# The first block of x loaded with two tokens per partition, and the token order restored by strided copies

## The chip, the cores and the metric

The kernel is one program on one core of a Trainium2 chip. The core has a matrix engine (PE in the profile, with its weight loads shown apart as PEld), a vector engine (DVE), a scalar engine with function tables (ACT), a general engine (POOL) and a sequencer that mostly issues transfers (SP). Sixteen DMA engines move data between the chip's memory (HBM) and the on-chip buffer. The metric is the device time of one execution in microseconds (us).

## The reference

One input x of 2048 tokens by 512 features goes through two branches, and a gate per token mixes them.

```python
x = A_x
g = _sigmoid((x * gate_w).sum(-1, keepdims=True))
a = _A_ref(x, A_wq, A_wk, A_wv, A_wo, A_beta)          # 32 heads of 16, four segments of 512 tokens
b = _B_ref(x, B_w_gate, B_w_up, B_w_down)              # gelu(x @ w_gate) * (x @ w_up) @ w_down, 1792 wide
return g * a + (1 - g) * b
```

Branch A is causal attention inside each segment of 512 tokens, plus a linear memory that each later segment reads from the segments before it. Branch B is a gated feed-forward layer. All inputs are bf16.

## The kernel before, in words

The tokens are worked in four segments (0 to 3) of 512. For a segment the kernel needs x with features on the partitions (the tile `xT`), from which the matrices K, Q, V, the gate product G and the up product U are made; attention is made of score matmuls (`qk`), exponentials on ACT (`exp`, of 128x2048 each), masks on POOL (`msk`) and value matmuls (`pv`); the down products (`D`, `R`) end a segment, and `fin` scales and stores.

Segments 1 to 3 get `xT` by transposing transfers. Segment 0 gets it in another way, because it is the start of the program: two transfers `x0_0` and `x0_1` (line 622) bring 256 tokens each into `xin`, a part of the tile `hT[1]`, with tokens on the partitions. Slot `a` of partition `p` holds token 256u + 128a + p. PE transposes the 128x128 pieces (`x0t0a_u`, `x0t0b_u`, `x0t1_u`, line 648) into PSUM, and three copies for each u (`x0ev0a_u`, `x0ev0b_u`, `x0ev1_u`, lines 653 to 656) put them into `xT[0]`: `x0ev0a_0`, `x0ev0a_1` and `x0ev1_0` run on DVE, the other three on ACT. The weights of K come meanwhile in three pieces: `w_wk0` and `w_wk1` from ACT's queue, `w_wk2` from SP's.

While the first transfers are on their way, PE runs eight matmuls on constants (`warm0` to `warm7`, line 639), seven of 512 columns and one of 256. Then come the transposes and the K matmuls of segment 0, which are cut so that a matmul needs one feature block and one half of the tokens (`K0_t.i`).

`xin` has a second use. `gmul0` (DVE) multiplies it by the gate weights, and `gsum0_0` to `gsum0_3` (lines 813 to 819) sum over the features: slot `a` gives the gate logits of 128 tokens in column `a` of `glog`. `gexs0` (ACT) takes the exponential, `gts0` (DVE) makes the reciprocal that `fin` scales with, `exsT0` (POOL, 16 small copies) puts it where `GdT0` (DVE) needs it, and `norm0_t` (DVE) scales the attention output with that.

The order of the work is written out by hand: the dictionary `ORDER` has one list of task names for each engine and one for SP's transfers, and each engine works through its list strictly. A task is given to ACT or to DVE by the list it stands in. A planner inside the kernel (`Sched`) walks the lists to assign PSUM banks and derives from the tasks' reads and writes which semaphores each instruction waits for. Its table `LANDING` holds the landing times that it assumes for the first transfers.

Of the kernel before, what the change touches and what calls it, by code (L numbers as in the profile page):

```python
# [13 lines left out]
ALU = mybir.AluOpType  # L14
# [80 lines left out]
    ),  # L95
    "act": (
# [370 lines left out]
def _build(es, nc, A_x, A_wq, A_wk, A_wv, A_wo, A_beta, B_w_gate, B_w_up, B_w_down, gate_w, out):  # L467
# [165 lines left out]
    xdma(1, 3, 4)  # L633
    wdma(("wg", 1), SP, wg[:, :, half:DF], wgr[:, :, half:DF], 1100000)

    for i in range(8):
        gw = Grp(banks)
        n = 256 if i == 7 else 512
        task(f"warm{i}", PE, [Instr(lambda e, gw=gw, n=n: e.matmul(  # L639
# [626 lines left out]
```

## Time and profile before

| quantity | value |
|---|---|
| time, median of 3 executions | 261.67 us |
| the three executions | 261.67, 906.1 and 261.62 us |
| span of the profiled execution | 657.2 us (10358 instructions) |
| busy on DVE, ACT, POOL in it | 190.9, 213.9 and 100.9 us |
| bytes moved in it | 18.43 MB in 32780 packets |

The span runs from the first to the last instruction of one execution that the profiler recorded; the page gives no other time for that execution. It is not an execution like the two near 261.6 us. Whatever is read off PE's rows therefore has to be brought to the pace of the median, while transfers and the other engines have their own clocks. In the views that follow, an instruction's row has its start, its duration, its engine, its line, the operation and its operands; `x8` at the end counts merged instructions. In rows of groups, the numbers behind the bar are busy us and the mean ns of one. In rows of stretches (such as 3.00:4.00) the last two numbers are the share of the 16 DMA engines that is busy and the GB/s that they move.

### The profile page before, as it was taken

Reading aid. Unit: us, or ns where it says so; the run is one execution under the profiler, and the core shown is the slowest. Engines: PE = TensorE matmul, PEld = TensorE weight load, DVE = VectorE, ACT = ScalarE, POOL = GpSimd, SP = SyncE. Lnnn points to the kernel's source line nnn. Section 1 sums busy time; section 2 is a strip of 40 time slices with the busy share of each in tenths; the row PEclk is TensorE's granted clock in tenths of the full one; section 3 lists DMA queues with packets and bytes.
Section 4 is the critical chain, followed back from the end, with each engine's and each line's share of the span. In section 5 each row is a group of like instructions: output and inputs, shape, how many; then the busy total and the mean of one; then the engine's idle time right before and its main releaser. Section 6 shows DMA issues by size and latency. Waiting matters only on the chain.

```text
span 657.2 us, 10358 instructions
## 1 busy us (share of the span) xinstructions
PE 654.3 (100%) x4644; PEld 225.9 (34%) x4644; DVE 190.9 (29%) x353; ACT 213.9 (33%) x184; POOL 100.9 (15%) x260
## 2 busy tenths in 40 slices
PE   9999999999999999999999999999999999999998
PEld 5222432323332323432332332334234233242344
DVE  0333344433333003442522003334432100233221
ACT  2434334347204223334224223334421332232210
POOL 4014024030003011213000110120220002203100
DMA  9000401000600300200001201001000000200001
GB/s 267 14 6 20 137 17 49 1 1 1 177 0 17 50 1 9 50 0 1 1 17 33 33 1 36 7 1 41 1 9 17 1 1 0 58 9 1 1 1 33
DMA packets 32780, 18.43 MB, mean 28 GB/s; under 512 B 20576, under 2 KB 32736, under 8 KB 32736
## 3 DMA queue, kind: packets, MB, share of 16 engines
q1 hardware_dynamic: 31904, 16.99, 10.6%
q10 hardware_dynamic: 832, 0.79, 0.4%
q8 instruction: 36, 0.59, 0.4%
q14 instruction: 8, 0.07, 0.0%
HBM read 9.84 MB, written 2.10 MB: 18 GB/s over the span
## 4 chain that ended last, share of the span: by engine, by line
PE 100%; DVE 0%; issue 0%
PE psW L545 39%; PE psW L547 26%; PE psW L1092 15%; PE psXALL L924 7%; PE psW L972 6%; PE psXALL L547 2%; PE psW L980 2%; PE psXALL L545 1%; PE psW L639 1%; PE psXALL L648 0%; PE psW L890 0%; PE psXALL L843 0%; DVE obf L1158 0%
## 5 line engine op out<-in xcount | busy, mean ns | idle before, releaser
L930 ACT ACTIVATE pt<-psXALL 128x2048 bf16<-128x2048 f32 x64 | 120.2, 1878 | 257.7 <-PE psXALL L924 254.0
L933 POOL TENSOR_SCALAR_AFFINE_SELECT pt<-pt 128x256 bf16<-128x256 bf16 x128 | 54.1, 431 | 366.2 <-ACT pt L930 361.7
L1092 PE MATMUL psW<-wd,hT 32*128 32x512 bf16 x576 | 90.3, 827 | 0.0
L545 PE MATMUL psW<-xT,wu 128*128 128x512 bf16 x122 | 76.3, 819 | 0.0
L545 PE MATMUL psW<-xT,wg 128*128 128x512 bf16 x118 | 74.3, 827 | 0.0
L1071 DVE TENSOR_TENSOR hT<-psW,hT 128x512 bf16<-128x512 f32 x56 | 38.2, 690 | 122.6 <-PE psW L545 69.5
L547 PE MATMUL psW<-xT,wg 128*32 128x512 bf16 x424 | 65.8, 822 | 0.0
L547 PE MATMUL psW<-xT,wu 128*32 128x512 bf16 x408 | 64.2, 821 | 0.0
L924 PE MATMUL psXALL<-qT,kpad 32*128 32x320 bf16 (+3 forms) x512 | 46.2, 475 | 0.0
L986 DVE STREAM_TRANSPOSE tb<-psW 128x512 f32<-128x512 f32 x32 | 22.7, 714 | 80.4 <-PE psW L980 80.4
L972 PE MATMUL psW<-pt,vaug 128*17 128x192 bf16 (+3 forms) x512 | 46.0, 526 | 0.0
L1092 PEld LDWEIGHTS psW<-wd,hT 32*128 32x128 bf16 x576 | 27.5, 169 | 53.4 <-issue 52.9
L1121 DVE TENSOR_SCALAR ost<-psW,omgt 128x512 bf16<-128x512 f32 x10 | 7.5, 750 | 116.4 <-PE psW L545 106.4
L933 POOL TENSOR_SCALAR_AFFINE_SELECT ptl<-ptl 128x512 bf16<-128x512 bf16 x32 | 21.6, 676 | 115.6 <-ACT ptl L930 114.0
L972 PEld LDWEIGHTS psW<-pt,vaug 128*17 128x17 bf16 x512 | 25.4, 157 | 31.6 <-issue 26.7
L545 PE MATMUL psW<-wv,xT 128*128 128x512 bf16 x54 | 35.1, 810 | 0.0
L545 PEld LDWEIGHTS psW<-xT,wg 128*128 128x128 bf16 x118 | 18.9, 166 | 45.4 <-issue 41.8
L545 PEld LDWEIGHTS psW<-xT,wu 128*128 128x128 bf16 x122 | 18.8, 161 | 45.2 <-issue 44.1
L1055 ACT ACTIVATE hT<-psW 128x512 bf16<-128x512 f32 x28 | 16.5, 598 | 54.0 <-PE psW L547 40.2
L924 PEld LDWEIGHTS psXALL<-qT,kpad 32*128 32x128 bf16 x512 | 12.0, 111 | 60.5 <-issue 53.3
L547 PEld LDWEIGHTS psW<-xT,wg 128*32 128x32 bf16 x424 | 19.6, 166 | 32.3 <-issue 30.2
L547 PEld LDWEIGHTS psW<-xT,wu 128*32 128x32 bf16 x408 | 18.5, 159 | 32.6 <-issue 30.7
(124 smaller groups left out, 550.5 us busy)
## 6 DMA issues: line engine op xcount, KB each, us to landing
out_dram<-ost SPq DMA_DIRECT2D x15, 128.0 KB, 1.8
wg<-in_B_w_gate_dram SPq DMA_DIRECT2D x2, 896.0 KB, 6.9
wu<-in_B_w_up_dram SPq DMA_DIRECT2D x2, 896.0 KB, 6.0
wd<-in_B_w_down_dram SPq DMA_DIRECT2D x2, 896.0 KB, 7.2
phkt<-in_A_x_dram SPq DMA_DIRECT2D x3, 512.0 KB, 4.0
vlow<-vaug SPq DMA_DIRECT2D x8, 136.0 KB, 2.7
hT<-in_A_x_dram SPq DMA_DIRECT2D x2, 256.0 KB, 3.8
wo<-in_A_wo_dram SPq DMA_DIRECT2D x1, 512.0 KB, 4.0
```

Of the source, the lines that this page charges most:

```text
L545: return e.matmul(view(), lhsT, rhs, start=first, stop=last)
L547: r = e.matmul(view()[c:c + 32, :], lhsT[:, c:c + 32], rhs, start=first, stop=last, tile_position=(0, c))
L924: instrs.append(Instr(lambda e, g=g, lhs=lhs, rhs=rhs, c0=c0, ncol=ncol: e.matmul(X[g][:, c0:c0 + ncol], lhs(32 * g), rhs(32 * g), start=T ...
L930: exp_task(s, f"exp{s}_{t}{name}", [Instr(lambda e: e.activation(dst[:], XALL[:, :].rearrange("p (g c) -> p g c", g=4), ACTF.Exp, scale=AT ...
L933: task(f"msk{s}_{t}{name}", POOL, [Instr(lambda e, view=view, pat=pat, base=base: e.affine_select(out=view, in_=view, compare_op=ALU.is_ge ...
L972: instrs.append(Instr(lambda e, t=t, q=q, kb=kb, slot=slot, c0=c0: e.matmul(gp.f32()[32 * q:32 * q + 17, 128 * kb + 64:512], Vaug[sl][:, k ...
L980: instrs.append(Instr(lambda e, t=t, q=q, kb=kb, c0=c0: e.matmul(gp.f32()[32 * q:32 * q + 17, 128 * kb:128 * kb + 64], Vlow[j][:, kb, 4 * ...
L986: task(f"pvt{s}_{t}_{j}", DVE, [Instr(lambda e: e.transpose(Tb[:, j, :], gp.f32()[:, :]), [gp.key], [("Tb", j)], 0.71)], grp=gp)
L1055: lambda e, g=g, ft=ft, s=s: e.activation(hT[s % 2][:, ft, :], g.f32()[:, :], ACTF.Gelu_apprx_tanh),
L1071: task(f"Um{s}_{ft}", DVE, [Instr(lambda e, g=g, ft=ft: e.tensor_tensor(hT[sl][:, ft, :], g.f32()[:, :], hT[sl][:, ft, :], ALU.mult), [g.k ...
L1092: return Instr(lambda e: e.matmul(gs[tile].f32()[:, :], a[32 * r:32 * r + 32, :], b[32 * r:32 * r + 32, :], start=False, stop=False, tile_ ...
L1121: DVE: [Instr(lambda e: e.tensor_scalar(ost[:], g.f32()[:, :], omgt[:, gt:gt + 1], None, ALU.mult), rd, wr, dve_t(512, ap=True))]}, grp=g))
```

## The change

- `x0_0` and `x0_1` put two consecutive tokens into each partition: slot `a` of partition `p` now holds token 256u + 2p + a. What a partition receives is then one run of 2 KB in HBM, where it was two runs of 1 KB.
- The six copies out of PSUM write with a step of two elements, so that `xT[0]` has its tokens in the old order.
- The gate sums of segment 0 go to spare columns 12 to 15 of `glog`. Four new transfers `gl00`, `gl01`, `gl10` and `gl11` on SP's queue, of 64 partitions by 2 single float32 values, bring them into columns 0 to 3 in the old order; `gexs0` waits for all four.
- The warm-up matmuls are seven of 512 columns; the one of 256 columns is gone.
- All five lists of `ORDER` are new. PE's list has the same tasks without `warm7`; SP's has the four new transfers. ACT's list gets 26 tasks that were on DVE and gives 17 to DVE. `LANDING` stays.

```diff
-            lambda u=u: A_x[0, u * 256:(u + 1) * 256, :].rearrange("(a p) d -> p a d", p=P), [],
+            lambda u=u: A_x[0, u * 256:(u + 1) * 256, :].rearrange("(p a) d -> p a d", p=P), [],
...
-    for i in range(8):
+    for i in range(7):
         gw = Grp(banks)
-        n = 256 if i == 7 else 512
-        task(f"warm{i}", PE, [Instr(lambda e, gw=gw, n=n: e.matmul(
-            gw.f32()[:, 0:n], ones[:, 0:128], ones[:, 0:n], start=True, stop=True),
-            [], [gw.key], mm_t(n))], grp=gw, bias=5000.0 - i)
+        task(f"warm{i}", PE, [Instr(lambda e, gw=gw: e.matmul(
+            gw.f32()[:, :], ones[:, 0:128], ones[:, :], start=True, stop=True),
+            [], [gw.key], mm_t(512))], grp=gw, bias=5000.0 - i)
...
-        dst = xT[0][:, k0:k0 + nk, 256 * u:256 * u + 256]
+        dst = xT[0][:, k0:k0 + nk, 256 * u:256 * u + 256].rearrange("p k (c a) -> p k a c", a=2)
...
-            DVE: [Instr(lambda e, dst=dst, src=src: e.tensor_copy(dst, src), [key], wr, dve_t(256 * nk, 2))]}))
+            DVE: [Instr(lambda e, dst=dst, src=src: e.tensor_copy(dst, src.rearrange("p k (a c) -> p k a c", a=2)), [key], wr, dve_t(256 * nk, 2))]}))
...
+        gl, gk = (glog[:, 12:16], ("glog", 3)) if s == 0 else (glog[:, s4], ("glog", s))
...
+                DVE: [Instr(lambda e, a=a: e.tensor_reduce(gl[:, a:a + 1], xt[:, a, :], AXX, ALU.add),
...
+        if s == 0:
+            for h in range(2):
+                for a in range(2):
+                    dma(f"gl{h}{a}", SP, lambda h=h, a=a: glog[a:P:2, h:4:2],
+                        lambda h=h, a=a: glog[64 * h:64 * h + 64, 12 + a:16:2],
+                        [gk + (c,) for c in (a, 2 + a)], [("glog", 0, h, a), ("glog", 0, 2 + h, a)], 60000, nonc=True)
```

The lists of ACT and SP in the part of segment 0 that has the gate's tasks, before and after:

```diff
 act
-Q0_3ev K0_2ev exp0_0A0 gexp K0_3ev exp0_0B0 Vev0_2 exp0_0L gsum0_1 exp0_0A1 Q1_1ev exp0_0B1 Q1_3ev gexs0
-exp0_1A0 pke0_1 exp0_1B0 Gev1_2 exp0_1A1 pqe1_0 exp0_1B1
+Q0_3ev kl0_11 exp0_0A0 Vev0_3 Vev0_2 exp0_0B0 Vev0_1 exp0_0L gexp gsum0_0 exp0_0A1 Q1_2ev exp0_0B1 pke0_1 exp0_1A0
+Q1_0ev exp0_1B0 gexs0 pqe1_0 exp0_1A1 pqe1_1 exp0_1B1
 sp
-w_wg1 Vlo0_1 Vlo0_0 pkT0_0 pkT0_2 pkT0_1 pkT0_3 w_wu0 w_wu1
+w_wg1 gl11 pkT0_0 Vlo0_1 gl01 gl10 Vlo0_0 gl00 pkT0_1 pkT0_3 pkT0_2 xt1 w_wu0 w_wu1
```

More of the change, by code (lines that the diff above doesn't have):

```diff
@@ L651, in _build @@
             for k in range(nk) for a in range(2)])
-        dst = xT[0][:, k0:k0 + nk, 256 * u:256 * u + 256]
+        dst = xT[0][:, k0:k0 + nk, 256 * u:256 * u + 256].rearrange("p k (c a) -> p k a c", a=2)
         wr = [("xT", 0, k0 + k, u) for k in range(nk)]
         S.add(Task(f"x0ev{nm}_{u}", {
-            ACT: [Instr(lambda e, dst=dst, src=src: e.activation(dst, src, ACTF.Copy), [key], wr, act_t(256 * nk))],
-            DVE: [Instr(lambda e, dst=dst, src=src: e.tensor_copy(dst, src), [key], wr, dve_t(256 * nk, 2))]}))
+            ACT: [Instr(lambda e, dst=dst, src=src: e.activation(dst, src.rearrange("p k (a c) -> p k a c", a=2), ACTF.Copy), [key], wr, act_t(256 * nk))],
+            DVE: [Instr(lambda e, dst=dst, src=src: e.tensor_copy(dst, src.rearrange("p k (a c) -> p k a c", a=2)), [key], wr, dve_t(256 * nk, 2))]}))
     c = [Instr(lambda e: e.memset(maskc[0][:], 0.0), writes=[("c", "mask", 0)], est=0.1)]
@@ L815, in prep @@
                 ACT: [Instr(lambda e, a=a: e.activation(xt[:, a, :], xt[:, a, :], ACTF.Copy,
-                                                        accum_out=glog[:, 4 * s + a:4 * s + a + 1]),
-                            [("gprod", s)] + xkeys, [("glog", s, a), ("gjunk", s, a)], 0.64)],
-                DVE: [Instr(lambda e, a=a: e.tensor_reduce(glog[:, 4 * s + a:4 * s + a + 1], xt[:, a, :],
-                                                           AXX, ALU.add),
-                            [("gprod", s)] + xkeys, [("glog", s, a), ("gjunk", s, a)], dve_t(512))]}))
+                                                        accum_out=gl[:, a:a + 1]),
+                            [("gprod", s)] + xkeys, [gk + (a,), ("gjunk", s, a)], 0.64)],
+                DVE: [Instr(lambda e, a=a: e.tensor_reduce(gl[:, a:a + 1], xt[:, a, :], AXX, ALU.add),
+                            [("gprod", s)] + xkeys, [gk + (a,), ("gjunk", s, a)], dve_t(512))]}))
+        if s == 0:
[4 more added lines that the diff above has]
+                        [gk + (c,) for c in (a, 2 + a)], [("glog", 0, h, a), ("glog", 0, 2 + h, a)], 60000, nonc=True)
         exp_task(ph, f"gexs{s}", [Instr(lambda e: e.activation(exs[:, s4], glog[:, s4], ACTF.Exp),
-                                        [("glog", s, a) for a in range(4)], [("exs", s)], 0.25)])
+                                        [("glog", s, a) + u for a in range(4)
+                                         for u in (((0,), (1,)) if s == 0 else ((),))], [("exs", s)], 0.25)])
         task(f"gts{s}", DVE, [
```

186 rows, old and new, of the table ORDER are left out of this document.

## The prediction

> **What bounds the kernel now.** The page came first, for the span and the engines' shares.
>
> ```profile
> span 657.2 us, 10358 instructions
> ...
> PE 654.3 (100%) x4644; PEld 225.9 (34%) x4644; DVE 190.9 (29%) x353; ACT 213.9 (33%) x184; POOL 100.9 (15%) x260
> ...
> PE 100%; DVE 0%; issue 0%
> ```
>
> The span, 657.2 us, is the only time of its own that the profile gives for this execution; nothing in it shows what lies around. It is 2.5 times the median, 261.67 us, and PE is busy for 654.3 us of it, which no run of 261.67 us can hold. So I take PE's rows at a smaller pace: 261.67 / 654.3 = 0.40 of their duration at most, if PE never rested in the median run. DVE's 190.9 and ACT's 213.9 us do fit into 261.67 (73 and 82%), so their rows and those of the transfers are used as they stand. The sum below is a difference: it is made on the profile's rows, and added to the median.
>
> Next I read the chain of work that ended last, and the timeline of the first microseconds, for what starts the real work.
>
> ```profile
> 0.85 4.58 PE psW L639 x8
> 5.44 1.11 PE psXALL L648 x8
> 6.54 1.48 PE psW L545 x5
> ...
> 28.56 5.94 PE psW L545 x10
> ```
>
> ```profile
> 0.82 0.96 SPq L582 DMA_DIRECT2D hT<-in_A_x_dram  x2
> ...
> 4.27 0.10 PEld L639 LDWEIGHTS psW<-const-bfloat16-1.0 128*128 128x128 bf16 x1 [0.39 <-issue]
> 4.89 1.34 PEld L648 LDWEIGHTS psXALL<-ident,hT 128*128 128x128 bf16 x8 [0.52 <-DMA hT<-in_A_x_dram]
> ```
>
> ```profile
> L582 SPq DMA_DIRECT2D hT<-in_A_x_dram x2: 450/452/454, 0.8 to 1.3; - x2
> ...
> DMA to landing us min/median/max: 3.5/3.8/4.1
> ```
>
> The first block was issued at 0.82 and landed 3.5 us later, at 4.3; the second at about 1.3 + 4.1 = 5.4. The trace puts the weight load at 4.89 down to that transfer, but it comes 0.62 us after the one at 4.27, as each warm-up's load does, and the warm-ups end at 5.43: in the profile PE, not the transfer, set the start. At 0.40 of their duration the warm-ups end by 0.85 + 4.58 x 0.40 = 2.7, and at twice that by 4.5. So in the median run the landing at 4.3, or the warm-ups very near it, starts the transposes. Everything behind them (K, scores, exponentials) follows in PE's order; time won there is won at the end unless a later wait takes it.
>
> **The packets.** The change makes 256 packets of 1 KB into 128 of 2 KB. No row has a 2-KB packet; the nearest are those of `w_g`, of 1.75 KB, alone on the engines at 15 to 17 us.
>
> ```profile
> 2.00:3.00 1.00, 1.00 (x3) 0.26 (x2) 0.00 (x0) 0.30 (x2) 0.85 (x4) 1.00 0.70 152
> 3.00:4.00 1.00, 1.00 (x3) 0.47 (x2) 0.00 (x0) 0.00 (x0) 1.00 (x1) 1.00 1.09 366
> 4.00:5.00 1.00, 1.00 (x3) 0.20 (x2) 0.00 (x0) 0.00 (x0) 1.00 (x2) 1.00 1.08 378
> ...
> 15.00:16.00 1.00, 1.00 (x4) 0.47 (x3) 0.00 (x0) 0.69 (x1) 0.00 (x0) 1.00 0.94 351
> 16.00:17.00 1.00, 1.00 (x3) 0.33 (x2) 0.00 (x0) 0.00 (x0) 0.00 (x0) 1.00 0.94 364
> ```
>
> With 1-KB packets the engines move 366 and 378 GB/s, with 1.75-KB ones 351 and 364: larger packets move no more bytes. The page "DMA: Bandwidth & Descriptors" of the Trainium skill (Specifications) speaks against this edit too: it asks for 512 B or more for line rate, so 1 KB is enough; by it alone the gain is nil, and the trace agrees.
>
> What can change is whose bytes go first. By 4.00 us 152 + 366 = 518 KB had moved, and `x0_0` is 262 of them; the other 256 KB (K's first weights, and part of what is behind) took 256 / 366 = 0.70 us of the engines. If all of it were to go behind `x0_0`, the block would land 0.7 us sooner; if none, no sooner. A loss I exclude, since the bytes and their rate stay. I take 0.2 us, nearer to nil, because the rate is the row that is known and the order among queues is not. The second block gains at least as much, or waits no longer; its landing at 5.4 lies behind the first K matmuls, so it must follow for the gain to hold, and it is in the same form.
>
> **The copies out of PSUM.** Six copies get a step of two elements.
>
> ```profile
> L656 DVE COPY xT<-psXALL 128x256 bf16<-128x256 bf16 x2 | 0.6, 292 | 8.2 <-PE psXALL L648 8.2
> L656 DVE COPY xT<-psXALL 128x512 bf16<-128x512 bf16 x1 | 0.4, 415 | 0.0
> L655 ACT ACTIVATE xT<-psXALL 128x256 bf16<-128x256 bf16 x2 | 0.8, 385 | 6.2 <-PE psXALL L648 6.2
> L568 DVE CAST qT<-psXALL 128x512 bf16<-128x512 f32 x1 | 0.7, 692 | 5.4 <-PE psXALL L545 5.4
> ```
>
> On DVE 256 more elements cost 415 - 292 = 123 ns, about 2 elements a ns, and the constant part is 169 ns. The nearest row that does not run so is the cast of 512, 692 ns: (692 - 169) / 512 = 1.02 ns an element. At that pace 256 elements take 169 + 261 = 430 ns and 512 take 692: 0.14 us more for `x0ev0a_0` and `x0ev0a_1` each, 0.28 for `x0ev1_0`. The least is nil. The page "VectorE: DVE Perf Modes" (What auto-detection actually checks) wants a step of one in every tensor for two elements a cycle, so by it the higher price is the right one. On ACT I book nothing: 385 ns for 256 elements is already slower than one a ns, so that a step has nothing to take away. The first copy is on the path (PE's first K matmul reads it); the later two have K's matmuls of the other half beside them, 1.48 us for five in the profile, still 0.6 us at 0.40. So 0.14 us is booked, with 0 and 0.14 + 0.14 + 0.28 = 0.56 as ends, the latter if that cover is gone.
>
> **The warm-up.** One matmul of 256 columns, 4.58 / 15 = 0.31 us in the profile, is gone. In the median run it ends before the block lands, so it is booked at nil; at the other end, where the warm-ups finish last, 0.31 x 0.40 = 0.12 us is won.
>
> **The gate.** Four transfers are new, and `gexs0` on ACT now waits for them; behind it are queued two phi exponentials and `exp0_1A1`, and the second next scores on PE wait for those.
>
> ```profile
> L930 ACT ACTIVATE pt<-psXALL 128x2048 bf16<-128x2048 f32 x64 | 120.2, 1878 | 257.7 <-PE psXALL L924 254.0 <-POOL exsT L830 3.7
> L748 ACT ACTIVATE pex<-kT 128x1024 bf16<-128x1024 bf16 x6 | 6.3, 1051 | 0.0
> L565 ACT ACTIVATE qT<-psW 128x512 bf16<-128x512 f32 x7 | 4.2, 597 | 24.4 <-PE psW L547 17.1 <-PE psW L545 7.4
> L830 POOL COPY exsT<-exs 32x4 f32<-32x4 f32 x64 | 13.7, 215 | 43.8 <-ACT exs L821 40.2
> ```
>
> ```profile
> 47.28 1.36 SPq L582 DMA_DIRECT2D vlow<-vaug  x2
> ```
>
> ```profile
> vlow<-vaug SPq DMA_DIRECT2D x8, 136.0 KB, 2.7
> ...
> gwb<-in_gate_w_dram SPq DMA_DIRECT2D x1, 128.0 KB, 7.3
> ```
>
> The last sum that they need is `gsum0_0`, on ACT. From there to `gexs0` ACT has four exponentials, one phi and two copies: 4 x 1.88 + 1.05 + 2 x 0.60 = 9.8 us. On SP's side there are three issues (`gl10`, `Vlo0_0`, `gl00`) at 1.36 / 2 = 0.68, and a landing: the nearest one, of small pieces on the same queue, is `vlow` with 2.7, so 4.7 us; with the slowest small load, 7.3 behind other loads, 9.3. Both are below 9.8, so the wait is booked at nil, with up to 1 us as its bad end. What SP's waiting holds up (`pkT0_1`, `w_wu0`) is not due sooner: `w_wu0` waits for `exp0_0B1` anyway, three ACT tasks after `gsum0_0`. `gexs0` itself moves behind two more exponentials; POOL's 16 copies, 16 x 0.215 = 3.4 us, then lie beside `exp0_1A1`, `exp0_1B1` and two phis, 2 x (1.88 + 1.05) = 5.9, before `norm0_0` needs them. If that cover went, up to 3.4 us of DVE's waiting would show.
>
> **The lists.** Up to the first exponential PE's list is the old one but for a swap inside K0. Later ACT takes over nine tasks net; I book nil, with the bounds below.
>
> Sum: -0.2 + 0.14 + 0 + 0 + 0 = -0.06, so 261.67 - 0.06 = **261.6 us**. Own range of this case: 261.0 (all of 0.7 won, no slower copy) to 262.2 (nothing won, 0.56 lost).
>
> **The rivals.** *More comes through*: the landing gains its full 0.7 us, or DVE, rid of nine tasks, was what PE waited for. For it: PE's order starts with that landing. Against it: DVE is at 73% of the median run. It gives 261.0, and in the extreme 9 x 0.69 = 6.2 us off, 255.5.
>
> *The packets change nothing*: no queue gives way, and only the slower copy is left: 261.8. For it speaks the equal rate.
>
> *ACT becomes the bound* (slower). It gets 26 tasks and gives 17; nine at the 0.597 of a copy are 5.4 us, and 213.9 + 5.4 = 219.3 us are 84% of the run. Segment by segment ACT's exponentials free the PSUM tile `psXALL` that the next scores need, and a copy ahead of one delays PE if PE is already there. Against it: in the profile ACT waits for PE for 254.0 us, though at PE's slow pace, and in the median run it still has 261.67 - 213.9 = 48 us of rest. It decides if more than half of the nine stand where ACT has none: 261.67 + 2.7 = 264.4, and 267.1 if all do.
>
> *The gate's transfers come late* (slower). If they take over 9.8 us, ACT stops: one exponential's worth is 261.67 + 1.88 = 263.5. Against it stand the 4.7 us.
>
> *PE's clock comes up later* (slower). The profile shows no ramp: warm-ups at 4.58 / 7.5 = 0.61 us a full matmul, later ones at 0.594, granted clock 1.00 throughout. If a shorter warm-up left K's 32 half matmuls at half pace, 32 x 1.48 / 5 x 0.40 / 2 = 1.9 us would be lost: 263.6. The page "TensorE: Matmul & The Clock Gate" (Part 1) has such a rule, a clock that doubles after some 3.4 us of activity; no row here shows it.
>
> *PE runs as in the profile* in most of the executions that make the new time: 657 us, for no reason in the change.
>
> **How the numbers follow.** Chances: forecast 0.46, more comes through 0.15, packets change nothing 0.12, ACT 0.13, gate 0.06, clock 0.04, PE's pace 0.04. The range of 260.8 to 263.8 leaves out about 0.05 of the first rival, 0.06 of ACT's, 0.04 of gate and clock, and PE's pace: 0.19. Two per cent, about what a measurement of this kernel can tell from no change, is 5.2 us. Faster by more asks for nearly all of DVE's nine tasks: 0.02. Slower by more are PE's pace, the upper end of ACT's rival (0.02) and of the gate's (0.01): 0.07. The rest, 0.91, is within.
>
> **What would show it.** In the new profile, the first block should land between 2.8 and 3.5 us after its issue (right with 3.3), with the GB/s of 3 to 5 us unchanged; `x0ev0a` should take about 430 ns on DVE and 385 on ACT; `gexs0` should have no wait for a transfer ahead of it, with the `gl` transfers landing in about 2.7 us. A wait of ACT on `glog`, or PE idle ahead of line 924 with ACT busy on copies, would make the forecast too low; a block that lands later than 3.5 us would make its first step wrong.

## The result, and the profile after

The changed kernel takes 262.57 us (median of six executions, 262.27 to 263.02), before 261.7 us beside it: a ratio of 1.0034, with a 95% interval of 1.0023 to 1.0046. The change costs 0.9 us, a third of a per cent, where 0.06 us of gain was forecast.

The profiled execution of the changed kernel took 262.68 us, 1.3 of them around its span. From its page, the span, the busy time of each engine, and the shares of the chain that ended last:

```profile
span 261.4 us, 10370 instructions
...
PE 257.7 (99%) x4643; PEld 125.9 (48%) x4643; DVE 183.2 (70%) x344; ACT 214.5 (82%) x195; POOL 104.4 (40%) x260
...
PE 95%; ACT 2%; POOL 1%; issue 0%; DVE 0%; ACTq 0%
```

The profile that the prediction had to use was of an execution in which PE was two and a half times slower. The kernel before was therefore profiled again, in an execution of 262.1 us. The same part of that page:

```profile
span 260.9 us, 10334 instructions
...
PE 253.8 (97%) x4620; PEld 126.9 (49%) x4644; DVE 188.5 (72%) x353; ACT 209.6 (80%) x184; POOL 106.5 (41%) x260
...
PE 94%; DMA 1%; DVE 1%; issue 1%; ACT 1%; ACTq 0%
```

(24 of PE's records are missing from that one, which is why it shows less of PE's time.) ACT took over 4.9 us of work and DVE lost 5.3. Neither engine is near the span; PE is. A microsecond that PE spends waiting is therefore a microsecond of the result, unless PE would have had to wait later anyway.

**A ruler that leaves the start out.** The start of the program, called the head here, varies between executions by several tenths of a microsecond (below), as much as the effect that is looked for. In before's order what follows it does not. Line 930 (936 after) issues 72 exponentials on ACT, each of which waits for scores from PE. The first and the last of them, from the timelines; a row has start, duration, engine, line, operation, operands, and in brackets the idle time before it with what ended it. Before:

```profile
14.17 1.88 ACT L930 ACTIVATE pt<-psXALL 128x2048 bf16<-128x2048 f32 x1
...
248.17 1.88 ACT L930 ACTIVATE pt<-psXALL 128x2048 bf16<-128x2048 f32 x1 [0.77 <-PE psXALL L924]
```

After:

```profile
14.01 1.88 ACT L936 ACTIVATE pt<-psXALL 128x2048 bf16<-128x2048 f32 x1
...
248.63 1.88 ACT L936 ACTIVATE pt<-psXALL 128x2048 bf16<-128x2048 f32 x1 [0.71 <-PE psXALL L930]
```

Before needs 248.17 - 14.17 = 234.00 us for this stretch, after needs 234.62. The changed kernel starts its exponentials 0.16 us sooner and ends them 0.46 us later: it loses 0.62 of its 0.9 us where neither the load nor the copies nor the warm-up have anything left to do. In all five profiles in the table below that have before's order of work unchanged, the stretch is 233.99 to 234.00 us, whatever was changed in the head.

**Where it goes.** The changed kernel's list of PE's waits has one that before's has not (line, what was waited for: us in total, times, longest):

```profile
PE psW L978 <- POOL pt L939: 0.4, 1, 0.4
```

The timeline and the chain of work around it, first the timeline's rows of ACT, POOL and PE, then the chain's (start, duration, what; left out are rows of 0.04 to 0.06 us between them):

```profile
105.60 1.89 ACT L936 ACTIVATE pt<-psXALL 128x2048 bf16<-128x2048 f32 x1
113.56 1.88 ACT L936 ACTIVATE pt<-psXALL 128x2048 bf16<-128x2048 f32 x1
115.50 4.83 POOL L939 TENSOR_SCALAR_AFFINE_SELECT pt<-pt 128x256 bf16<-128x256 bf16 x8 [2.34 <-ACT pt L936]
119.09 0.61 PE L978 MATMUL psW<-pt,vaug 128*17 128x448 bf16 x16 [0.40 <-POOL pt L939]
```

```profile
113.56 1.89 ACT pt L936
...
115.50 0.42 POOL pt L939
...
115.98 0.79 POOL pt L939 x2
...
116.83 1.65 POOL pt L939 x2
...
118.54 0.51 POOL pt L939
...
119.09 0.61 PE psW L978 x16
```

POOL masks the exponentials of group 2 of the heads in segment 1 here, two selects for each of them (four for 2L), before PE may use them. The group is the second digit of the names; the kernel numbers four such groups, and the expectations below call them key blocks. `pv1_2_0` needs 2A0, 2B0 and 2L, but not 2A1 and 2B1, which are for `pv1_2_1`. In its new list the order is `msk1_2L msk1_2B1 msk1_2B0 msk1_2A0 msk1_2A1`; ACT makes them in the order 2A0, 2B0, 2L, 2A1, 2B1. So POOL stands still for 2.34 us until the last, `exp1_2B1`, ends at 115.45, while 2B0's input has been ready since 105.60 + 1.89 = 107.5. Then it takes 2B1's two selects first, and only the sixth of the row, which ends at 119.05, lets PE go. The same place before:

```profile
104.65 0.97 POOL L933 TENSOR_SCALAR_AFFINE_SELECT pt<-pt 128x256 bf16<-128x256 bf16 x2 [1.71 <-ACT pt L930]
110.13 3.16 POOL L933 TENSOR_SCALAR_AFFINE_SELECT ptl<-ptl 128x512 bf16<-128x512 bf16 x4 [4.51 <-ACT ptl L930]
113.24 0.90 POOL L933 TENSOR_SCALAR_AFFINE_SELECT pt<-pt 128x256 bf16<-128x256 bf16 x2
115.42 3.75 POOL L933 TENSOR_SCALAR_AFFINE_SELECT pt<-pt 128x256 bf16<-128x256 bf16 x6 [1.28 <-ACT pt L930]
...
117.62 0.61 PE L972 MATMUL psW<-pt,vaug 128*17 128x448 bf16 x16
```

There the order is `msk1_2A0 msk1_2L msk1_2B0 msk1_2B1 msk1_2A1`: 2A0's two selects come at 104.65, 2L's four at 110.13 and 2B0's two at 113.24, so that all that `pv1_2_0` needs is ready at 114.14. POOL also waits for `exp1_2B1`, but behind that, and PE comes to `pv1_2_0` at 117.62 without a wait.

**The head**, on which the prediction had spent its words: the timeline of the changed kernel, the landing of the two transfers of the block, counted from their issue (the minimum is `x0_0`'s), and the groups of the copies.

```profile
0.85 3.15 PE L638 MATMUL psW<-const-bfloat16-1.0 128*128 128x512 bf16 x7 [0.85 <-PEq L1257]
4.00 1.03 PE L647 MATMUL psXALL<-ident,hT 128*128 128x128 bf16 x8
4.94 1.25 PE L545 MATMUL psW<-xT,wk 128*128 128x256 bf16 x5
...
9.56 3.19 PE L545 MATMUL psXALL<-xT,wq 128*128 128x512 bf16 x14
...
DMA to landing us min/median/max: 3.1/3.5/3.9
...
L655 DVE COPY xT<-psXALL 128x256 bf16<-128x256 bf16 x2 | 0.9, 448 | 6.0 <-PE psXALL L647 6.0
...
L654 ACT ACTIVATE xT<-psXALL 128x256 bf16<-128x256 bf16 x2 | 0.9, 458 | 3.9 <-PE psXALL L647 3.9
```

Before, at the same pace:

```profile
4.67 1.03 PE L648 MATMUL psXALL<-ident,hT 128*128 128x128 bf16 x8 [0.46 <-DMA hT<-in_A_x_dram]
5.50 1.01 PE L545 MATMUL psW<-xT,wk 128*128 128x256 bf16 x5
...
DMA to landing us min/median/max: 3.8/4.2/4.6
```

The transposes start at 4.00 instead of 4.67, but the exponentials only 0.16 us sooner: PE gave the rest back between, in matmuls that in this execution ran at a slower pace until about 6 us. That is told of in the last section.

### The profile page after: what moved, and what is told of

Its sections match the earlier page's. It is cut to its first block, busy times and chain, and to the rows that moved or that the text cites. A ratio compares the mean times of both kernels' runs of the same rounds, so it can differ in the third digit from the quotient of the medians.

```text
span 261.4 us, 10370 instructions
## 1 busy us (share of the span) xinstructions
PE 257.7 (99%) x4643; PEld 125.9 (48%) x4643; DVE 183.2 (70%) x344; ACT 214.5 (82%) x195; POOL 104.4 (40%) x260
## 4 chain that ended last, share of the span: by engine, by line
PE 95%; ACT 2%; POOL 1%; issue 0%; DVE 0%; ACTq 0%
PE psW L545 35%; PE psW L547 24%; PE psW L1098 14%; PE psXALL L930 9%; PE psW L978 6%; PE psXALL L547 2%; ACT pt L936 1%; PE psW L986 1%; PE psXALL L545 1%; POOL pt L939 1%; PE psW L638 1%; ACT ptl L936 1%; PE psW L896 1%; PE psXALL L849 1%; PE psXALL L647 1%
## 5 line engine op out<-in xcount | busy, mean ns | idle before, releaser
L1098 PE MATMUL psW<-wd,hT 32*128 32x512 bf16 x576 | 34.9, 374 | 0.0
L545 PE MATMUL psW<-xT,wu 128*128 128x512 bf16 x118 | 29.9, 380 | 0.0
L545 PE MATMUL psW<-xT,wg 128*128 128x512 bf16 x116 | 28.6, 380 | 0.0
L547 PE MATMUL psW<-xT,wu 128*32 128x512 bf16 x424 | 26.1, 380 | 0.0
L547 PE MATMUL psW<-xT,wg 128*32 128x512 bf16 x432 | 26.1, 379 | 0.0
L930 PE MATMUL psXALL<-qT,kpad 32*128 32x320 bf16 (+3 forms) x512 | 25.6, 272 | 0.3 <-ACT ptl L936 0.2
L978 PE MATMUL psW<-pt,vaug 128*17 128x192 bf16 (+3 forms) x512 | 19.3, 273 | 0.4 <-POOL pt L939 0.4
L836 POOL COPY exsT<-exs 32x4 f32<-32x4 f32 x64 | 14.1, 220 | 7.9 <-ACT exs L826 4.2
L936 ACT ACTIVATE ptl<-psXALL 128x2048 bf16<-128x2048 f32 x8 | 15.0, 1879 | 2.5 <-PE psXALL L930 2.5
L978 PEld LDWEIGHTS psW<-pt,vaug 128*17 128x17 bf16 x512 | 11.8, 91 | 10.4 <-POOL pt L939 1.5
```

What stands on the lines that cost most here:

```text
L545: return e.matmul(view(), lhsT, rhs, start=first, stop=last)
L547: r = e.matmul(view()[c:c + 32, :], lhsT[:, c:c + 32], rhs, start=first, stop=last, tile_position=(0, c))
L836: cross = task(f"exsT{s}", POOL, [Instr(lambda e, g=g, c=c: e.tensor_copy(exsT[sl][32 * g:32 * g + 32, c:16:4], exs[32 * c:32 * c + 32, s4 ...
L930: instrs.append(Instr(lambda e, g=g, lhs=lhs, rhs=rhs, c0=c0, ncol=ncol: e.matmul(X[g][:, c0:c0 + ncol], lhs(32 * g), rhs(32 * g), start=T ...
L936: exp_task(s, f"exp{s}_{t}{name}", [Instr(lambda e: e.activation(dst[:], XALL[:, :].rearrange("p (g c) -> p g c", g=4), ACTF.Exp, scale=AT ...
L978: instrs.append(Instr(lambda e, t=t, q=q, kb=kb, slot=slot, c0=c0: e.matmul(gp.f32()[32 * q:32 * q + 17, 128 * kb + 64:512], Vaug[sl][:, k ...
```

## The experiments

Theory: the new lists hold the loss, and in them the five masks just shown. Rivals: the load, the copies or the shorter warm-up cost more than booked. All were timed in five rounds beside before, whose own median was 261.82 us beside e0 to e3, 261.69 beside e4 to e7 and 261.62 beside f1 to f4; so it is the ratios that can be compared, rather than the medians. "Stretch" is first to last exponential, read as above from each kernel's timeline.

| kernel | median, us | ratio to before (95%) | first exponential | stretch | PE's waits for POOL, us |
|---|---|---|---|---|---|
| before again (e0) | 262.02 | 1.0004 (0.9995 to 1.0013) | 14.17 | 234.00 | none |
| new lists alone (e1) | 262.57 | 1.0031 (1.0021 to 1.0041) | 13.63 | 234.65 | 0.4 |
| load alone (e2) | 261.60 | 0.9988 (0.9979 to 0.9997) | 13.34 | 233.99 | none |
| one warm-up fewer (e3) | 261.73 | 0.9997 (0.9988 to 1.0006) | 13.79 | 234.00 | none |
| e1, old masks (e4) | 261.95 | 1.0017 (1.0008 to 1.0027) | 14.36 | 234.22 | none |
| new lists, then old (e5) | 262.43 | 1.0028 (1.0017 to 1.0040) | 13.68 | 234.88 | none |
| old lists, then new (e6) | 263.26 | 1.0064 (1.0052 to 1.0076) | 14.13 | 235.45 | 1.1 |
| load, one warm-up fewer (e7) | 261.47 | 0.9996 (0.9988 to 1.0004) | 13.29 | 234.00 | none |
| the change, old masks (f1) | 262.04 | 1.0014 (1.0003 to 1.0024) | 13.79 | 234.26 | none |
| before, new masks (f2) | 263.36 | 1.0066 (1.0054 to 1.0078) | 13.60 | 235.59 | 1.4 |
| e7, straight copies (f3) | 261.57 | 0.9998 (0.9989 to 1.0006) | 13.46 | 234.00 | none |
| the change, old POOL list (f4) | 265.11 | 1.0144 (1.0124 to 1.0163) | 13.91 | 238.70 (some 1.5 too long, see f4) | 2.2 |

### The change taken apart

e0 is before, unchanged, for a profile at the pace of the median.

> The kernel before, unchanged, for a profile at the pace of the median: ratio 1.000 within 0.001, span about 260.4 us (its 261.7 less the 1.3 us that lay around the span of the changed kernel). Lists theory: it has less idle time of PE behind the first 14 us than the changed kernel, by 0.9 us. Load theory: the difference of 0.9 us is there by the first scores, at 13.5 us in the changed kernel.

It is before's time again, so that 0.1% is what five rounds can tell here.

e1 has the new lists and nothing else of the change but the warm-up that they lack:

```diff
 ORDER = {
-    (before's five lists)
+    (the change's five lists, without gl00 to gl11)
...
-    for i in range(8):
+    for i in range(7):
```

> The new lists alone (seven warm-ups, the four gate copies taken out of the list), with the old load and the plain copies out of PSUM. Lists theory: 262.4 to 262.7, ratio 1.003. Load theory: 261.6 to 261.8, ratio 1.000.

e2 is the opposite: before's lists and its eight warm-ups, with the two-token load, the strided copies and the four gate transfers:

```diff
-            lambda u=u: A_x[0, u * 256:(u + 1) * 256, :].rearrange("(a p) d -> p a d", p=P), [],
+            lambda u=u: A_x[0, u * 256:(u + 1) * 256, :].rearrange("(p a) d -> p a d", p=P), [],
...
-w_wg1 Vlo0_1 Vlo0_0
+w_wg1 gl11 gl01 gl10 gl00 Vlo0_1 Vlo0_0
```

> The old lists and the eight warm-ups, with the load of two tokens per partition, the strided copies out of PSUM and the four gate copies (put right ahead of the value transfers on SP's queue). Lists theory: 261.5 to 261.8, ratio 1.000. Load theory: 262.4 to 262.7, ratio 1.003.

e3 takes `warm7` from before:

```diff
-"warm0 warm1 warm2 warm3 warm4 warm5 warm6 warm7 x0t0a_0
+"warm0 warm1 warm2 warm3 warm4 warm5 warm6 x0t0a_0
```

> The kernel before without the eighth warm-up, nothing else. Both theories: 261.7, ratio 1.000, since the first block lands after the warm-ups. A theory that PE's clock comes up later with a shorter warm-up: 262.2 or more.

As the lists theory had it, the lists alone cost what the whole change costs (1.0031 against 1.0034), and lengthen the stretch by 0.65 us. The load alone gains 0.2 us, by an interval that just leaves out nothing; the warm-up does nothing that can be measured. e7 puts load and shorter warm-up together on before's lists, which is the whole change but for its order of work:

```diff
-"warm0 warm1 warm2 warm3 warm4 warm5 warm6 warm7 x0t0a_0
+"warm0 warm1 warm2 warm3 warm4 warm5 warm6 x0t0a_0
...
-w_wg1 Vlo0_1 Vlo0_0
+w_wg1 gl11 gl01 gl10 gl00 Vlo0_1 Vlo0_0
```

> Before's lists with the two-token load, the strided copies, the four gate copies and 7 warm-ups: the whole change but for its new order of work. If the parts add up: 261.8 - 0.2 (load) - 0.1 to 0 (warm-up) = 261.5 to 261.6 us, ratio 0.999. Rival, that the eighth warm-up is needed once the block lands sooner or later by its own jitter: 0.2 to 0.4 us above that, ratio 1.000 to 1.001.

261.47 us, ratio 0.9996: neither better nor worse than before, so it doesn't confirm e2's gain. It lies between what was expected (0.999) and the rival's 1.000 to 1.001, and between e7 and e2 the eighth warm-up can't be told from nothing.

### The masks

Three kernels reorder the same five names in POOL's list. e4 puts them back in e1, f1 in the whole change; f2 puts the new order into before and changes nothing else there.

```diff
 e4 and f1
-msk1_2L msk1_2B1 msk1_2B0 msk1_2A0 msk1_2A1
+msk1_2A0 msk1_2L msk1_2B0 msk1_2B1 msk1_2A1
 f2
-msk1_2A0 msk1_2L msk1_2B0 msk1_2B1 msk1_2A1
+msk1_2L msk1_2B1 msk1_2B0 msk1_2A0 msk1_2A1
```

> The new lists alone once more, with one stretch of POOL's list put back: the masks of key block 2 in segment 1 in before's order (msk1_2A0 first, msk1_2B0 ahead of msk1_2B1). Mask theory: in the new order POOL stands still for exp1_2B1 while the exponentials of 2B0 and 2A0 are long done, and PE's pv1_2 waits for the late masks; the start times of the exponentials jump by 0.59 us there, of which some 0.45 stays to the end. Then this gives back 0.35 to 0.55 us of the 0.75 that the lists cost: about 262.1 us, ratio 1.001 to 1.0018. Rival, that the loss is spread over the lists and the jump at this place would be made good by slack later: 262.5 to 262.6, ratio 1.003, as with the new lists alone.

> The whole change with one stretch of POOL's list put back: the five masks of key block 2 in segment 1 in before's order. Mask theory: from the first exponential to the end it takes some 247.0 us as the new lists with this order did, 0.45 less than the changed kernel's 247.4; PE waits for POOL nowhere; 262.57 - 0.45 = 262.1 us, ratio 1.0015. Rival, that the mask wait only hides another wait of the changed kernel: 262.5, ratio 1.003.

> Before with nothing changed but the order of these five masks on POOL (msk1_2L 2B1 2B0 2A0 2A1 in place of msk1_2A0 2L 2B0 2B1 2A1). Mask theory: a wait of PE for POOL of 0.4 us (as in the new lists) to 1.1 us (as in the hybrid with before's lists ahead of it) appears at pv1_2, and the time grows by about as much: 262.1 to 262.9 us, ratio 1.0015 to 1.004. Rival, that PE has slack to take it up: 261.7 us, ratio 1.000.

e4 and f1 came out as the mask theory had it (1.0017 and 1.0014). f1 gives 0.5 us back (1.0034 to 1.0014), and its stretch falls from 234.62 to 234.26. Counted from the first exponential, its exponentials start within 0.01 us of the changed kernel's up to `exp1_3B0`, the last one ahead of `pv1_2_0`; from `exp1_3B1` on f1 is 0.30 to 0.37 us ahead, 0.36 at the end. Its timeline at the place has 2B0's two selects at 112.89, then the four of 2B1 and 2A1, and PE at `pv1_2_0` without a wait:

```profile
112.89 1.22 POOL L938 TENSOR_SCALAR_AFFINE_SELECT pt<-pt 128x256 bf16<-128x256 bf16 x2
115.27 2.61 POOL L938 TENSOR_SCALAR_AFFINE_SELECT pt<-pt 128x256 bf16<-128x256 bf16 x4 [1.16 <-ACT pt L935]
...
118.39 0.61 PE L977 MATMUL psW<-pt,vaug 128*17 128x448 bf16 x16
```

f2 is the plainest of all. 2A0, 2L and 2B1 changed places, 2B0 and 2A1 kept theirs, and it takes 1.7 us more:

```profile
114.84 5.45 POOL L931 TENSOR_SCALAR_AFFINE_SELECT pt<-pt 128x256 bf16<-128x256 bf16 x10 [2.13 <-ACT pt L928]
...
118.64 0.61 PE L970 MATMUL psW<-pt,vaug 128*17 128x448 bf16 x16 [1.42 <-POOL pt L931]
```

POOL's wait for ACT is about that of the changed kernel (2.13 and 2.34 us), but PE comes to `pv1_2_0` 1.42 us ahead of its masks, not 0.40. So the change's own lists make up for most of what its mask order costs. By which of their moves is not shown: the new PE list has `pv1_2_0` behind `qk1_3B0` where before's has it ahead, but so has e6 below, and it waits 1.1 us. And the stretch of f2, 235.59, is 1.59 us over before's: a wait of 1.42 us is still there in full at the last exponential, and nothing downstream takes any of it up. Expected were 0.4 to 1.1 us of wait, and 262.1 to 262.9 us; the mechanism was right and its price too low.

f4 takes the whole of before's POOL list into the changed kernel:

```diff
     "pool": (
-        (the change's list)
+        (before's list)
```

> The whole change with before's whole list for POOL in place of its own; the lists of the other engines stay new. If the masks of key block 2 in segment 1 are POOL's whole part in the loss, it comes out as with these five alone put back, 262.1 us, ratio 1.0015; if others of POOL's moves cost too, below that, towards 261.7 and 1.000; if the new POOL list suits the new order of the other engines elsewhere, above it, 262.3 or more.

```profile
31.89 4.58 POOL L835 COPY exsT<-exs 32x4 f32<-32x4 f32 x16 [4.71 <-ACT exs L825]
...
39.51 4.30 POOL L938 TENSOR_SCALAR_AFFINE_SELECT pt<-pt 128x256 bf16<-128x256 bf16 x10
...
43.02 0.66 PE L977 MATMUL psW<-pt,vaug 128*17 128x320 bf16 x12 [1.33 <-POOL pt L938]
```

265.11 us, the third of the outcomes that were named, and well beyond the 262.3 put to it. In the changed kernel `gexs0` stands later on ACT than before. Both POOL lists have `exsT0`, which waits for it, ahead of the masks of group 1 in segment 0; but before's list has `omg` and `consts` between the two, and the new one has them earlier, where POOL is idle. The same place in the changed kernel:

```profile
31.81 4.59 POOL L836 COPY exsT<-exs 32x4 f32<-32x4 f32 x16 [2.53 <-ACT exs L826]
36.47 4.00 POOL L939 TENSOR_SCALAR_AFFINE_SELECT pt<-pt 128x256 bf16<-128x256 bf16 x8
```

In f4 the masks begin at 39.51 instead of 36.47, and PE stands at them for 1.33 us; two more waits for POOL, of 0.29 us just ahead and of 0.62 us at 137 us, make up the 2.2 of the table. Here, then, the new list suits the new order of ACT; at `msk1_2` it does not.

The profiled execution of f4 has something more. It took 266.63 us, the other four 264.86 to 265.24, and behind the wait PE's granted clock (the third number from the end) is shown at half for some three microseconds:

```profile
42.00:43.00 1.00, 0.00 (x0) 0.00 (x0) 0.00 (x0) 0.42 (x1) 0.93 (x4) 1.00 0.45 95
43.00:44.00 1.00, 0.98 (x32) 0.69 (x36) 0.06 (x1) 0.00 (x0) 0.93 (x3) 0.52 0.97 319
...
45.00:46.00 1.00, 1.00 (x28) 0.26 (x24) 0.96 (x2) 0.00 (x0) 0.77 (x4) 0.50 1.05 398
46.00:47.00 1.00, 1.00 (x31) 0.53 (x20) 0.93 (x3) 0.53 (x1) 0.86 (x3) 0.77 1.07 382
```

In the other four the mean clock is 1.000, so the median doesn't have this; the stretch of 238.70 does, and is longer than the median's by about 266.63 - 265.11 = 1.5 us.

### Two hybrids

e5 has the new lists up to `exp1_2A0` and before's from there on, e6 the reverse. ACT's list at the seam, where the one gives way to the other:

```diff
 e5, against the new list
-exp1_2A0 Vev2_0 fin0_3 exp1_2B0 exp1_2L
+exp1_2A0 fin0_3 exp1_2B0 Q2_2ev Vev2_0 exp1_2L
 e6, against before's list
-exp1_2A0 fin0_3 exp1_2B0 Q2_2ev Vev2_0 exp1_2L
+exp1_2A0 Vev2_0 fin0_3 exp1_2B0 exp1_2L
```

> The new lists up to the exponential of key block 2 in segment 1 (some 105 us into the span), before's lists from there on; the load and the copies as before, 8 warm-ups. Mask theory: only the loss ahead of that place is in it, 0.2 to 0.3 us by the start times of the exponentials: 262.0 to 262.1 us, ratio 1.001. Rival of a loss in the head or in segment 0 alone: the whole 0.75, 262.5.

> The counterpart: before's lists up to that place, the new lists from there on (the changed mask order is in it). Mask theory: 0.4 to 0.5 us of loss, 262.2 to 262.3 us, ratio 1.0017, and POOL's mask group waiting 2.3 us for ACT as in the new lists. Rival of a loss in the head or in segment 0 alone: nothing, 261.8.

Both missed: the halves cost 0.88 and 1.45 us of stretch, the whole 0.65. e5's 262.43 us is near what the rival of a loss in segment 0 had named (262.5), but by accident: counted from the first, `exp1_2A0` starts 0.09 us later than before's, and `exp1_2A1`, three exponentials on and behind the seam, 0.87 us later. They don't say where the new lists lose, because each brings a seam of its own: e5 has a wait of PE's value product for DVE of 0.3 us that neither parent has, and e6's old first half brings PE to `pv1_2_0` 1.1 us ahead of its masks. What e6 does add is another size of the same wait. The stretch beyond before's 234.00, with PE's wait for POOL in brackets: e4 0.22 (none), e1 0.65 (0.4), e6 1.45 (1.1), f2 1.59 (1.4).

### The strided copies

f3 is e7 with the copies out of PSUM written straight; the tokens of the first block then stay in the order of the load, so segment 0 comes out in another order.

```diff
-        dst = xT[0][:, k0:k0 + nk, 256 * u:256 * u + 256].rearrange("p k (c a) -> p k a c", a=2)
+        dst = xT[0][:, k0:k0 + nk, 256 * u:256 * u + 256]
```

> The change without its new lists (before's order of work, 7 warm-ups), and the copies out of PSUM written straight instead of to every second token: the tokens of each half of segment 0's first block stay in the order in which they were loaded, so its output is in another order there. Strided copies as I booked them: DVE's first copy falls from 448 ns back to 300 to 320, ACT's from 458 to 385, and the time by 0.14 us or a little more, 261.3 us, ratio 0.999. Rival, that the strides cost nothing on the path: 261.47, ratio 0.9996.

Groups of the copies in f3:

```profile
L655 DVE COPY xT<-psXALL 128x256 bf16<-128x256 bf16 x2 | 0.6, 290 | 5.4 <-PE psXALL L647 5.4
...
L654 ACT ACTIVATE xT<-psXALL 128x256 bf16<-128x256 bf16 x2 | 0.8, 384 | 3.2 <-PE psXALL L647 3.2
```

The copies themselves get faster by 448 - 290 = 158 ns on DVE and 458 - 384 = 74 ns on ACT. The time doesn't show it: 0.9998 against e7's 0.9996, as the rival had it. With intervals of 0.1% a price of up to 0.2 us on the path can't be excluded.

## Why the prediction was right or wrong

**Wrong: "The lists".** The forecast failed in one short step: "Later ACT takes over nine tasks net; I book nil". It measured +0.75 us by e1 (262.57 against 261.82 beside it), and no other part of the change, timed without it, showed a cost. So the time came out above before's, where 0.06 us of gain was forecast; 262.57 lies within the range of 260.8 to 263.8, but above the 262.2 at which the case's own range ends. The reason given for looking at the lists at all, ACT's load, was not the one that mattered: ACT went from 209.6 to 214.5 us, and the changed kernel's longest wait of PE for ACT is 0.2 us, at the same line as before's. The rival "ACT becomes the bound" fell with it. The missed piece was a queue on which no task was added or moved between engines: POOL's. A list may change in its order alone, and the prediction counted only the tasks that changed engines. Both orders stand in the kernels' lists: POOL's masks could have been held against ACT's exponentials, place by place.

**Not wholly settled.** The masks explain 0.36 us of the changed kernel's 0.62 us of stretch (234.62 to 234.26 in f1). Between e1 and e4 it is 0.43 of 0.65, but 0.18 of that stands there before the masks' place, where the two have the same lists, so that tenths of a microsecond vary in the new order. The other 0.26 us shows no wait of PE that the lists of waits have and before's lacks. Most of it lies in the matmuls themselves: within the stretch PE is busy, by the profiles, for 233.68 us in e7 and 233.86 in f1, over 4254 matmuls in both. No run tells which moves that comes from, nor where the 0.3 us of the loss lie that are outside the stretch; the head varies by more than that.

**The packets.** The block lands sooner, as forecast, and by more; the reason given is not shown. Signs named were 2.8 to 3.5 us after the issue, right with 3.3; it was 3.1, against 3.8 in before's profile at the median's pace, and 3.1 to 3.2 in all six profiles with this load against 3.5 to 3.8 in the others. So 0.3 to 0.7 us come through where 0.2 was booked, near the other bound. The total shows less: e2's 0.9988 is 0.2 to 0.3 us off, e7's 0.9996 and f3's 0.9998 some 0.1 or less. The rate of the engines was to stay unchanged:

```profile
2.00:3.00 1.00, 1.00 (x4) 0.35 (x3) 0.00 (x0) 0.29 (x2) 0.85 (x4) 1.00 0.79 196
3.00:4.00 1.00, 1.00 (x3) 0.09 (x2) 0.00 (x0) 0.00 (x0) 1.00 (x1) 1.00 1.08 381
4.00:5.00 1.00, 1.00 (x9) 0.83 (x10) 0.45 (x1) 0.35 (x1) 1.00 (x2) 1.00 1.05 372
```

The last column is GB/s. From 3 to 5 us it is 381 and 372, where the prediction's rows had 366 and 378: unchanged. More was moved between 2 and 3 us, 196 against 152. So part of the gain may be an earlier start of the bytes (the two issues take 385 and 417 ns, in e0 449 and 455), and not the order among queues on which the prediction rested; no run here parts the two. A price that was not booked shows as well: in f1 PE waits 0.24 us for K's weights. The slowest of their three pieces landed 4.5 to 5.6 us after its issue in the profiles with this load, 4.6 to 4.9 in those at the same pace without. The rule cited there from the page "DMA: Bandwidth & Descriptors" of the Trainium skill (Specifications), that 512 B is enough for line rate, fits these equal rates. It does not price a landing, and the measured one decides against reading it as no gain.

**The copies.** DVE was sized well at its upper price: 430 ns forecast for 256 elements, 448 measured. ACT was not: 385 forecast as unchanged, 458 measured, so a step of two slows it by a fifth. In the time neither shows, and the 0.14 us booked stays below what f3 can see.

**The gate.** Right. The four transfers landed 2.0 us after their issue (2.7 forecast), and `gexs0` started without a wait. Of the cover for POOL's 16 copies a little went: DVE waits 0.6 us for them once. From the table of transfers and ACT's timeline:

```profile
glog<-glog SPq DMA_DIRECT2D x4, 0.5 KB, 2.0
```

```profile
31.55 0.20 ACT L826 ACTIVATE exs<-glog 128x4 f32<-128x4 f32 x1
```

**The warm-up.** Nil was right within what e3 and e7 can tell.

## What to carry to other kernels

When a change brings new lists of work for in-order queues, compare the order on each queue with the order in which its inputs are made, also on queues whose tasks are all the same as before; one wrong neighbour here cost 0.4 us in the changed kernel and 1.7 in f2, more than the load won. On PE, busy 99% of the span, the wait was paid in full at the end (1.42 us waited and 1.59 lost in f2), so a list of such an engine's waits, before and after, is the first thing to read. And when an edit and a new order come together, time each alone: in before's order the edit of the load is worth 0.0 to 0.3 us (ratios 0.9988, 0.9996 and 0.9998), and each of these kernels comes out better than the whole change (1.0034).

## What the runs showed of the hardware

PE's pace in the head. In the changed kernel's head, quoted above, seven warm-up matmuls of 512 columns take 3.15 us, 0.45 each; fourteen of 512 columns at 9.56 take 3.19, 0.23 each. Five matmuls of 256 columns at 4.94 take 1.25 us; in e7, which has the same warm-ups and load, they take 0.72:

```profile
3.92 0.80 PE L647 MATMUL psXALL<-ident,hT 128*128 128x128 bf16 x8
4.85 0.72 PE L545 MATMUL psW<-xT,wk 128*128 128x256 bf16 x5
```

So PE starts at half its pace and reaches the whole at some 3.5 to 6.7 us into the span, not at the same moment in each execution: f2's eight warm-ups take 3.12 us and e0's 3.36, so that f2's last ones are fast already, while in e4 two transposes at 6.24 us still take 0.42 us, where e0's at 6.34 take 0.28. The granted clock is shown as 1.00 in each of these microseconds. The prediction had rightly found no such ramp in its profile, where all ran slowly, and gave it little weight. The page "TensorE: Matmul & The Clock Gate" of the Trainium skill (Part 1) has a clock that doubles after some 3.4 us of activity; the trace agrees with the doubling, and puts it at some 2.7 to 5.9 us after the first warm-up at 0.85. It has two consequences. An earlier block can find PE still at half pace: 0.67 us at the start of the transposes gave 0.16 at the first exponential between the profiles of before and after, but 0.88 (13.29 against 14.17) in e7, where PE was faster sooner. And the first exponential of an unchanged kind of head moves by over half a microsecond between executions (13.60 in f2, 14.17 in e0, which have the same head). Whatever is to be measured below that has to be measured past the head.

The clock can fall again later. In the execution of f4 quoted above the granted clock went to 0.50 behind a rest of PE of 1.33 us and was back at 1.00 in the fifth microsecond; f2's rest of 1.42 us was followed by 1.00 throughout. So a wait of that length doesn't always bring it, and no run here shows what decides.
